# Attention and two MLPs on one core: the transposes of the units that Pool splits stand one step later in SP's order, and the softmax weights get a fifth buffer

## The chip, the core and the metric

The kernel runs on one core of a Trainium2 chip. Six instruction streams work side by side and meet at semaphores: PE (matrix multiplications, with PEld for its weight loads), DVE (vector work), ACT (activations, and DMAs that it issues), POOL (vector work on a third engine) and SP, which in this kernel only issues DMAs. Each stream keeps its order: an instruction that waits holds up all that stands behind it in the same stream. The metric is the time of one execution on the device in microseconds, the median of the runs.

## The reference

Three stages follow each other: attention with a learned bias on the scores, an MLP with the largest of three products, and a gated MLP. Sizes: 4 batches, 8 heads, 576 positions, head size 64; 2304 tokens of 512; inner sizes 768 and 1536.

```python
scores = scale * np.matmul(q, k.transpose(0, 1, 3, 2))
scores = scores + bias.transpose(2, 0, 1)[None, :, :, :]
scores = scores - np.max(scores, axis=-1, keepdims=True)
attn = np.exp(scores)
attn = attn / (np.sum(attn, axis=-1, keepdims=True) + 1e-09)
attn_out = np.matmul(attn, v)
h = np.maximum(np.maximum(x @ w1, x @ w2), x @ w3)   # x: attn_out, heads side by side
x = h @ w_out
gate = 1.0 / (1.0 + np.exp(-(x @ w_gate)))
out = gate * (x @ w_val) @ w_out2
```

## The kernel before, in words

Precision comes from pairs of 16-bit numbers: a float32 value is scaled and split into a high part `hi` and a rest `lo`, and a product takes three matmuls (`mm3`, L797).

**Units and steps.** The 32 heads go in 16 pairs P. A pair has 10 units: five row tiles (four of 128 rows, one of 64) for each of its two heads, alternating. Unit u has position u mod 10 in its pair: position 0 and 1 are tile 0 of the two heads, 2 and 3 tile 1, and so on. The loop over `u` makes one step for each unit, and every step emits work for units of different age. For unit x: scores on PE (`emit_S`, L617 and L618), at step x the sum with the bias and the row's maximum on DVE (`emit_E`, L637) and the exponential on ACT (`emit_X`, L643), at x+1 the reciprocal of the row's sum, then the split. In between the step issues a load of bias rows on ACT's DMA queue (`load_bias`, L519, for unit u+3), takes some products of the first MLP of the batch before (`feed`, L797, with their evacuation on ACT at L818 and on DVE at L820) and prepares later pairs (`prep`: loads of q, k, v, their split, the transposes of q and k by DMA at L411 and the swapped copy of k on DVE at L421 and L422). Order is thus written out by hand: each engine gets its instructions in the order in which the steps emit them.

**The split of the softmax weights.** From unit 40 on, the weights of a unit are split into a buffer `ph` (128 rows, twice 576 numbers of 16 bits); there are `NPH` buffers. For most units ACT writes `hi` at step x+1 (`emit_hi`, L662) and DVE writes `lo` at x+2 (`emit_lo`, L677). For the units at positions 2 and 5 (and 8 as well for units below 80) Pool does the float32 work (`by_pool`): it scales the row at x+1 (L659), ACT copies `hi` at x+2 (`emit_hi2`, L668) and Pool subtracts at x+3 (L674). These 28 units are called Pool's units here, the other 92 plain.

**The transpose T(x).** A full `ph` is turned by one DMA transpose on SP into `pt` (`emit_T`, L702): at step x+2 for a plain unit, at x+4 for one of Pool's. When it has landed, the `ph` buffer is free. Buffers are handed out in the order in which the program released them. The product with v (`emit_V`, L756) reads `pt`: units 0 to 3 of a pair at step 11 counted from the pair's first unit, units 4 to 9 at step 15.

Before unit 40 none of this is used (PE transposes there), and after the loop come the rest of the first MLP and the whole gated MLP (L1177 to L1217).

Of the kernel before, what the change touches and what calls it, by code (L numbers as in the profile page):

```python
# [13 lines left out]
BF16 = mybir.dt.bfloat16  # L14
# [14 lines left out]
FIRST_MOE = 6  # L29
OUT_AT = 6  # L30
QLEAD, QEARLY = 16, 6
NBI, NPH, NE, NVH = 3, 4, 4, 4
ESC = 16384.0
DOWN = 2.0 ** -15
DOWN2 = 2.0 ** -15
# [29 lines left out]
def tile_kernel(ctx, tc, q, k, v, w1, b1, w2, mw1, mw2, mw3, mwo, gw, vw, ow, xtab, masks, out):  # L65
# [3 lines left out]
    F1 = mw1.shape[1]  # L69
# [91 lines left out]
    with tc.manual_schedule():  # L161
# [8 lines left out]
        wpool = wp1.enter_context(tc.tile_pool(name="wpool", bufs=1))  # L170
# [1 line left out]
        hT = wpool.tile([128, 2, K1, S], F16, tag="hT", name="hT")  # L172
        xTs = [wpool.tile([128, 2 * KC, S], F16, tag=f"xT{i}", name=f"xT{i}") for i in range(2)]
        mt = wp1.enter_context(tc.tile_pool(name="mt", bufs=2))
        junk_v = wpool.tile([128, 640], BF16, tag="junk_v", name="junk_v")
        junk_x = junk_v[:, :S]
        junk_w = wpool.tile([128, F1], BF16, tag="junk_w", name="junk_w")


        def w_in(i):  # L180
# [330 lines left out]
        bias_t, e_t, ph_t, l_t, r_t, pt_t = {}, {}, {}, {}, {}, {}  # L511
# [133 lines left out]
        def emit_r1(u):  # L645
            m = rows[units[u][1]]
            r_t[u] = p4.tile([128, 1], F32, tag="r", name="r")
            nc.vector.tensor_scalar(r_t[u][:m], l_t.pop(u)[:m], 1e-9, 1.0 / ESC, op0=ALU.add, op1=ALU.mult)

        def by_pool(u):  # L650

            return u % 10 in ((2, 5, 8) if u < 20 * PPB else (2, 5)) and not by_pe(units[u][0])
# [42 lines left out]
        def emit_T(u):  # L695
            n, it = units[u]
            m = rows[it]
            g, i0 = (0, 0) if it < 2 else (1, 2)
            if it == i0:
                pt_t[n, g] = p1.tile([128, 9, (256, 320)[g]], F16, tag=f"pt{g}{n % 2}", name="pt")  # L700
            c0 = 128 * (it - i0)
            nc.sync.dma_start_transpose(out=pt_t[n, g][:, :, c0:c0 + m], in_=ph_t.pop(u)[:m].rearrange("p a s -> p (a s)"))  # L702
# [222 lines left out]
        def at_step(u, off):  # L925
            return [u - off] if 0 <= u - off < NU else []

        for u in range(NU + 7):
# [23 lines left out]
            tiny()  # L952
            for x in at_step(u, 1):
                emit_r1(x)
            for x in at_step(u, 4):
                if by_pool(x):
                    emit_T(x)
            for x in at_step(u, 2):
                emit_hi2(x)
                if not (by_pe(units[x][0]) or by_pool(x)):  # L960
                    emit_lo(x)
                    emit_T(x)
# [311 lines left out]
```

## Time and profile before

| | us |
|---|---|
| median of 3 runs | 1090.01 (1089.54 to 1098.89) |
| the profiled execution | 1105.99 |
| its span, first to last instruction | 1104.2 |
| units 40 to 159 with their tails (185 to 590 us of the span) | 405.0 |
| rest of the first MLP and gated MLP (590 us to the end) | 514.2 |
| PE busy in the whole span | 1001.4 (91%) |
| DVE busy | 691.0 (63%) |
| ACT busy | 550.3 (50%) |
| POOL busy | 190.5 (17%) |

A row of the timeline gives the start, the duration, the engine, the line, the operation with the tiles it writes and reads, and in brackets how long the engine sat idle before it and what ended that. An engine name with a q (SPq, ACTq) marks an instruction of the issuing stream, such as the issue of a DMA.

### The profile page before, as it was taken

The page shows a single profiled execution, that of the slowest core. Times are in us where ns is not written, and L with a number is a line of the kernel's source. Part 1 is how long each engine was busy: PE and PEld are TensorE (multiplying, and loading weights), DVE is VectorE, ACT ScalarE, POOL GpSimd, SP SyncE. Part 2 cuts the span into 40 slices and gives each one's busy share as a digit, 9 for nine tenths or more (in the row PEclk, how much of TensorE's full clock was granted, in tenths as well). Part 3 has the DMA queues.
Part 4 walks back from the last instruction along what each step waited for, and adds up shares of the span by engine and source line. Part 5 has one row for each costly group of instructions (what it writes and reads, how often), then busy time and mean ns, then how long its engine had stood idle before and what let it go on. Part 6 is the DMA issues. An engine that isn't in the chain of part 4 may idle for free.

```text
span 1104.2 us, 20184 instructions
## 1 busy us (share of the span) xinstructions
PE 1001.4 (91%) x7620; PEld 660.0 (60%) x7620; DVE 691.0 (63%) x1764; ACT 550.3 (50%) x1089; POOL 190.5 (17%) x199
## 2 busy tenths in 40 slices
PE   5977899778987889987999998998999999999998
PEld 2223454556664566655777776777764676777753
DVE  6997878888976887876884876778620221222210
ACT  6998778657675666765664435544410111111100
POOL 1003454434432233212330110000000000000000
PEclk9999999999898998988999999999999999999999
DMA  7898979999999999979994332323001000000001
GB/s 212 295 264 235 207 201 220 263 220 195 209 202 196 200 201 186 250 170 194 183 172 121 105 112 61 113 94 116 2 1 39 11 20 11 10 11 10 11 20 39
DMA packets 242957, 148.53 MB, mean 135 GB/s; under 512 B 183084, under 2 KB 214060, under 8 KB 242860
## 3 DMA queue, kind: packets, MB, share of 16 engines
q1 hardware_dynamic: 221472, 104.76, 45.5%
q10 hardware_dynamic: 21388, 42.48, 14.5%
q8 instruction: 60, 0.98, 0.4%
q14 instruction: 37, 0.30, 0.1%
HBM read 89.53 MB, written 15.34 MB: 95 GB/s over the span
## 4 chain that ended last, share of the span: by engine, by line
PE 52%; DVE 20%; DMA 12%; ACT 7%; issue 6%; POOL 1%; SPq 1%; ACTq 1%; DVEq 0%; POOLq 0%
PE po L1212 13%; PE mm L797 12%; PE pg L797 8%; PE pvl L797 8%; DMA pt<-ph 7%; PE s L797 3%; PE s L617 3%; DVE xT L543 2%; PE mm L756 2%; PE t L690 2%; ACT ph L662 2%; PE mm L752 1%; DVE e L637 1%; DVE gT L1187 1%; DVE wf L93 1%
## 5 line engine op out<-in xcount | busy, mean ns | idle before, releaser
L797 PEld LDWEIGHTS <-slot 128*128 128x128 f16 x2304 | 224.7, 101 | 106.1 <-issue 40.1
L797 PE MATMUL mm<-xT,slot 128*128 128x288 f16 x1512 | 220.8, 302 | 25.8 <-ACT hm L818 19.7
L1212 PE MATMUL po<-OW,gT 128*128 128x512 f16 x648 | 141.3, 379 | 0.0
L797 PEld LDWEIGHTS <-GW 128*128 128x128 f16 x1152 | 112.7, 98 | 41.7 <-issue 9.0
L797 PEld LDWEIGHTS <-VW 128*128 128x128 f16 x1152 | 112.2, 98 | 28.2
L643 ACT ACTIVATE e<-e,mx 128x576 f32<-128x576 f32 (+1 forms) x120 | 92.6, 771 | 45.4 <-DVE mx L637 39.0
L797 PE MATMUL pg<-x,GW 128*128 128x288 f16 x864 | 113.3, 288 | 0.5 <-DVE x_e L154 0.5
L797 PE MATMUL pvl<-x,VW 128*128 128x288 f16 x864 | 111.7, 286 | 0.0
L1212 PEld LDWEIGHTS <-gT 128*128 128x128 f16 x648 | 63.4, 98 | 74.8
L1177 ACT ACTIVATE sg<-pg,ug 128x576 f32<-128x576 f32 x48 | 35.5, 739 | 144.7 <-PE pg L797 131.1
L677 DVE SCALAR_TENSOR_TENSOR ph<-e,r,ph 128x576 f16<-128x576 f32 (+1 forms) x92 | 82.3, 895 | 39.1 <-ACT ph L662 38.9
L1184 DVE SCALAR_TENSOR_TENSOR sg<-pvl,sg 128x576 f32<-128x576 f32 x48 | 36.2, 754 | 108.5 <-PE pvl L797 107.6
L637 DVE CUSTOM_DVE_ANT_0 e<-s,bias 128x576 f32<-128x576 f32 (+1 forms) x120 | 89.4, 745 | 6.6 <-DMA bias<-bias_d 4.7
L662 ACT ACTIVATE ph<-e,r 128x576 f16<-128x576 f32 (+1 forms) x92 | 71.1, 773 | 32.9 <-DMA pt<-ph 26.0
L1186 ACT CAST gT<-sg 128x576 f16<-128x576 f32 x48 | 32.2, 672 | 107.4 <-DVE sg L1184 107.4
L617 PE MATMUL s<-k,kq 128*128 128x512 f16 (+1 forms) x160 | 63.9, 400 | 19.7 <-DVE k L422 19.7
L552 PE MATMUL bo<-xT,w2blk 128*32 128x512 f32 x192 | 61.2, 637 | 18.7 <-DVE xT L543 14.9
L617 PE MATMUL s<-kq 128*128 128x512 f16 (+1 forms) x160 | 64.9, 406 | 8.6 <-DVE mx L637 5.7
L1217 DVE TENSOR_TENSOR ob<-po,uo 128x512 f32<-128x512 f32 x16 | 11.1, 691 | 96.8 <-PE po L1212 96.8
L797 PE MATMUL mm<-hT,slot 128*128 128x288 f16 x504 | 66.2, 286 | 0.4 <-DVE xT L763 0.4
L826 POOL TENSOR_TENSOR hT<-hm,hT 128x576 f16<-128x576 f32 x24 | 39.2, 1632 | 113.3 <-ACT hT L825 105.9
L1187 DVE TENSOR_TENSOR gT<-sg,gT 128x576 f16<-128x576 f32 x48 | 36.4, 758 | 34.9 <-ACT gT L1186 34.9
(203 smaller groups left out, 1642.8 us busy)
## 6 DMA issues: line engine op xcount, KB each, us to landing
bias<-bias_d ACTq DMA_DIRECT2D x128, 288.0 KB, 3.9
bias_d<-x SPq DMA_DIRECT2D x36, 288.0 KB, 4.7
x<-in_moe_w_dram SPq DMA_DIRECT2D x12, 768.0 KB, 7.2
w<-in_moe_w_gate_dram SPq DMA_DIRECT2D x12, 512.0 KB, 3.7
w<-in_moe_w_val_dram SPq DMA_DIRECT2D x12, 512.0 KB, 3.6
w<-in_moe_w_out_dram SPq DMA_DIRECT2D x12, 512.0 KB, 3.4
bias<-bias_d ACTq DMA_DIRECT2D x32, 144.0 KB, 4.9
out_dram<-ob SPq DMA_DIRECT2D x36, 128.0 KB, 2.3
```

What stands on the lines that cost most here:

```text
L552: nc.tensor.matmul(bo[32 * g:32 * g + 32, 0:512], lhsT=lhsT, rhs=hs[4 * ti + g][:, :, 0:128], start=True, stop=True, tile_position=(0, 32 ...
L617: nc.tensor.matmul(ps[:m, 0:512], lhsT=qs, rhs=kk[:, 0:4], start=(j == 0), stop=(j == 1))
L637: nc.vector.tensor_tensor_reduce(e[:m], ps[:m, :S], bias_t.pop(u)[:m], -1.0, 3.0e38, ALU.add, ALU.min, mx[:m])
L643: nc.scalar.activation(e_t[u][:m], e_t[u][:m], AF.Exp, scale=-1.0, bias=x_t.pop(u)[:m], accum_out=l_t[u][:m])
L662: nc.scalar.activation(ph_t[u][:m, 0], e_t[u][:m], AF.Copy, scale=r[:m])
L677: nc.vector.scalar_tensor_tensor(ph[:m, 1], e_t.pop(u)[:m], r_t.pop(u)[:m], ph[:m, 0], op0=ALU.mult, op1=ALU.subtract)
L797: nc.tensor.matmul(ps[hf][:, :HS], lhsT=W(wp, kk), rhs=X(xp, kk)[:, hf * HS:(hf + 1) * HS], start=(first and i == 0), stop=(last and i == 2))
L826: nc.gpsimd.tensor_tensor(hT[:, 1, m], hm, hT[:, 0, m], op=ALU.subtract)
L1177: nc.scalar.activation(hm3(sg), pg[:, :, :HS], AF.Sigmoid, scale=ugm)
L1184: nc.vector.scalar_tensor_tensor(hm3(sg), pvl[:, :, :HS], DOWN2, hm3(sg), op0=ALU.mult, op1=ALU.mult)
L1187: nc.vector.tensor_tensor(gT[:, 1, m, c0:c0 + S], sg, gT[:, 0, m, c0:c0 + S], op=ALU.subtract)
L1212: nc.tensor.matmul(po[:, 0, :], lhsT=gT[:, gi, kk, 128 * ct:128 * ct + 128], rhs=OW[:, wi, kk], start=(i == 0), stop=(i == 3 * K2 - 1))
```

## The change

Three edits. `NPH` goes from 4 to 5. The room comes from one area less for results that nobody reads: `junk_v` becomes a part of `junk_w`. And `emit_T` of Pool's units moves from step x+4 to x+5, still ahead of the plain transposes of its step. Because unit 7 now comes ahead of unit 5, the first of a `pt` buffer's units to be issued, whichever it is, takes the buffer.

```diff
-NBI, NPH, NE, NVH = 3, 4, 4, 4
+NBI, NPH, NE, NVH = 3, 5, 4, 4
@@
-        junk_v = wpool.tile([128, 640], BF16, tag="junk_v", name="junk_v")
+        junk_w = wpool.tile([128, F1], BF16, tag="junk_w", name="junk_w")
+        junk_v = junk_w[:, :640]
         junk_x = junk_v[:, :S]
-        junk_w = wpool.tile([128, F1], BF16, tag="junk_w", name="junk_w")
@@ in emit_T
-            if it == i0:
+            if (n, g) not in pt_t:
                 pt_t[n, g] = p1.tile([128, 9, (256, 320)[g]], F16, tag=f"pt{g}{n % 2}", name="pt")
@@ in the loop over u
-            for x in at_step(u, 4):
+            for x in at_step(u, 5):
                 if by_pool(x):
                     emit_T(x)
```

The order of PE, DVE, ACT and POOL is the same row by row. What moves is SP's order. First SP in pair 9 (units 90 to 99), steps 94 to 101. The buffers `ph_4536` (unit 92, Pool's), `ph_4539` (93), `ph_4585` (94), `ph_4688` (95, Pool's), `ph_4691` (96), `ph_4732` (97), `ph_4788` (98) and `ph_4836` (99) stand in this order before:

```order
L411 DMA_TRANSPOSE kq_4544<-R_4354 128x10x128
L702 DMA_TRANSPOSE pt_4495<-ph_4539 128x9x128
L359 DMA rqk_118<-in_k_dram 128x2x256
L360 DMA rqk_118<-in_k_dram 64x2x64
L411 DMA_TRANSPOSE kq_4621<-R_4354 128x10x128
L702 DMA_TRANSPOSE pt_4453<-ph_4536 128x9x128
L702 DMA_TRANSPOSE pt_4640<-ph_4585 128x9x128
L702 DMA_TRANSPOSE pt_4640<-ph_4691 128x9x128
L702 DMA_TRANSPOSE pt_4783<-ph_4688 128x9x128
L702 DMA_TRANSPOSE pt_4783<-ph_4732 128x9x128
L702 DMA_TRANSPOSE pt_4640<-ph_4788 128x9x64
```

And the same place now, where the buffers' numbers are lower by one or two (`ph_4535` is unit 92, `ph_4584` unit 94, `ph_4687` unit 95, `ph_4731` unit 97):

```order
L411 DMA_TRANSPOSE kq_4543<-R_4353 128x10x128
L702 DMA_TRANSPOSE pt_4494<-ph_4538 128x9x128
L359 DMA rqk_117<-in_k_dram 128x2x256
L360 DMA rqk_117<-in_k_dram 64x2x64
L411 DMA_TRANSPOSE kq_4620<-R_4353 128x10x128
L702 DMA_TRANSPOSE pt_4638<-ph_4584 128x9x128
L702 DMA_TRANSPOSE pt_4452<-ph_4535 128x9x128
L702 DMA_TRANSPOSE pt_4638<-ph_4690 128x9x128
L702 DMA_TRANSPOSE pt_4783<-ph_4731 128x9x128
L702 DMA_TRANSPOSE pt_4783<-ph_4687 128x9x128
L702 DMA_TRANSPOSE pt_4638<-ph_4786 128x9x64
```

T(92) has changed places with T(94), and T(95) with T(97); each Pool transpose is one place later and the plain one one place earlier. In pairs 4 to 7 T of position 8 moves in the same way behind T of the next pair's unit 0.

Second ACT in steps 98 and 99 of the same pair, with the semaphores that a row waits for (DMAHW: a DMA that has landed). Before:

```order
L662 ACTIVATE ph_4732<-e_4674,r_4727 128x576 [waits DMAHW6_49,DVE_49,Activation_49]
L818 ACTIVATE hm_4764<-mm_4662,fac_1850 128x288 [waits PE_49]
L818 ACTIVATE hm_4764<-mm_4667,fac_1850 128x288 [waits PE_49]
L643 ACTIVATE e_4767,l_4769<-e_4767,mx_4768 64x576 [waits DVE_49]
L519 DMA bias_4772<-bias_d_60 128x576 [waits DMAHW7_49,DMAHW5_49]
L662 ACTIVATE ph_4788<-e_4715,r_4781 64x576 [waits DVE_49,Activation_49]
```

and now:

```order
L662 ACTIVATE ph_4731<-e_4672,r_4726 128x576 [waits DMAHW1_49,DVE_49,Activation_49]
L818 ACTIVATE hm_4763<-mm_4660,fac_1849 128x288 [waits PE_49]
L818 ACTIVATE hm_4763<-mm_4665,fac_1849 128x288 [waits PE_49]
L643 ACTIVATE e_4766,l_4768<-e_4766,mx_4767 64x576 [waits DVE_49]
L519 DMA bias_4771<-bias_d_60 128x576 [waits DMAHW6_49,DMAHW5_49]
L662 ACTIVATE ph_4786<-e_4714,r_4780 64x576 [waits DVE_49,Activation_49]
```

The rows are the same; `hi` of unit 97 waits for another transpose than before (T(92) before, T(93) now), and the load of bias rows behind it waits in both for T(94), whose semaphore it takes over.

## Rows read from the trace of the kernel before

**Rows 1.** Windows view: engines' busy us (instructions), then PEclk, DMA share, GB/s.
```profile
185.00:590.00 405.00, 352.31 (x2920) 243.80 (x2919) 322.70 (x894) 263.92 (x561) 129.12 (x120) 0.93 1.05 200
590.00:1104.20 514.20, 499.06 (x3604) 348.82 (x3602) 216.61 (x472) 137.35 (x244) 9.10 (x6) 0.99 0.16 47
```
**Rows 2.** Waits view of PE, 185 to 590 us: total us, times, longest.
```profile
PE mm L797 <- ACT hm L818: 19.7, 6, 5.1
PE s L617 <- DVE k L422: 19.7, 13, 3.5
```
**Rows 3.** Waits view of ACT, same stretch.
```profile
ACT ph L662 <- DMA pt<-ph: 26.0, 14, 4.2
ACT ph L668 <- DMA pt<-ph: 8.8, 5, 2.6
```
**Rows 4.** Timeline, pair 9: Pool's subtraction of unit 92, T(92) and T(94).
```profile
365.51 1.28 POOL L674 TENSOR_TENSOR ph<-e,ph 128x576 f16<-128x576 f32 x1 [1.30 <-DMA bias<-bias_d]
374.54 3.42 SPq L702 DMA_TRANSPOSE pt<-ph  x1
378.06 2.56 SPq L702 DMA_TRANSPOSE pt<-ph  x1
```
**Rows 5.** Tile view of `pt`: all transposes T, min/median/max of issue in ns, then landing.
```profile
L702 SPq DMA_TRANSPOSE pt<-ph x120: 1199/1729/4258, 187.3 to 582.5; - x120
DMA to landing us min/median/max: 2.9/4.9/8.8
```
**Rows 6.** Timeline of ACT: eight writes of `hi` that waited for a buffer.
```profile
244.85 0.78 ACT L662 ACTIVATE ph<-e,r 128x576 f16<-128x576 f32 x1 [1.98 <-DMA pt<-ph]
309.52 0.78 ACT L662 ACTIVATE ph<-e,r 128x576 f16<-128x576 f32 x1 [1.54 <-DMA pt<-ph]
319.38 0.77 ACT L662 ACTIVATE ph<-e,r 128x576 f16<-128x576 f32 x1 [2.88 <-DMA pt<-ph]
343.13 0.77 ACT L662 ACTIVATE ph<-e,r 128x576 f16<-128x576 f32 x1 [2.44 <-DMA pt<-ph]
381.75 0.78 ACT L662 ACTIVATE ph<-e,r 128x576 f16<-128x576 f32 x1 [2.59 <-DMA pt<-ph]
415.23 0.77 ACT L662 ACTIVATE ph<-e,r 128x576 f16<-128x576 f32 x1 [4.21 <-DMA pt<-ph]
510.55 0.78 ACT L662 ACTIVATE ph<-e,r 128x576 f16<-128x576 f32 x1 [1.34 <-DMA pt<-ph]
518.06 0.77 ACT L662 ACTIVATE ph<-e,r 128x576 f16<-128x576 f32 x1 [3.62 <-DMA pt<-ph]
```
**Rows 7.** Timeline of PE: the idle time next behind each of those eight.
```profile
247.60 0.38 PE L617 MATMUL s<-k,kq 128*128 128x512 f16 x1 [2.79 <-DVE k L422]
312.27 0.38 PE L617 MATMUL s<-k,kq 128*128 128x512 f16 x1 [1.58 <-DVE k L422]
321.74 0.16 PE L130 MATMUL s<-vmx,ones 128*128 128x1 bf16 x1 [1.18 <-ACT junk_v L371]
346.12 3.18 PE L797 MATMUL mm<-xT,slot 128*128 128x288 f16 x12 [3.97 <-ACT hm L818]
382.96 1.90 PE L797 MATMUL mm<-xT,slot 128*128 128x288 f16 x12 [1.75 <-ACT hm L818]
416.45 3.19 PE L797 MATMUL mm<-xT,slot 128*128 128x288 f16 x12 [3.92 <-ACT hm L818]
513.72 0.38 PE L617 MATMUL s<-k,kq 128*128 128x512 f16 x1 [1.38 <-DVE k L422]
519.27 3.19 PE L797 MATMUL mm<-xT,slot 128*128 128x288 f16 x12 [4.36 <-ACT hm L818]
```
**Rows 8.** Timeline of ACT: the longest wait of a copy `hi` (Pool's unit), with the load ahead.
```profile
472.42 0.35 ACTq L519 DMA_DIRECT2D bias<-bias_d  x1
472.87 0.67 ACT L668 CAST ph<-e 128x576 f16<-128x576 f32 x1 [2.58 <-DMA pt<-ph]
```
**Rows 9.** Windows view, 5 us behind one of those idle times.
```profile
345.00:350.00 5.00, 3.88 (x15) 2.03 (x15) 3.90 (x17) 3.10 (x6) 0.68 (x1) 0.50 1.29 192
```

## The prediction

> **What bounds the kernel now.** I read the windows first. Between 185 and 590 us PE is busy 352.3 of 405.0 us, behind that 499.1 of 514.2 [rows 1]. The change touches only units from 40 on, so only the first of these stretches can move, and there PE is the busiest engine (DVE 322.7, ACT 263.9): PE sets the pace and loses 405.0 − 352.3 = 52.7 us by idling. The waits of PE say for whom: 19.7 us for ACT's evacuation of a product (L818) and 19.7 us for DVE's copy of k (L422) [rows 2]. Both are works that come late because something ahead of them on their engine was late. The waits of ACT show that something: 26.0 us in 14 writes of `hi` and 8.8 us in 5 copies `hi` of Pool's units, all for a transpose that still held the `ph` buffer, 34.8 us together [rows 3].
>
> Why is the transpose late? In pair 9 Pool ended unit 92 at 366.79 (365.51 + 1.28), but T(92) began only at 374.54 and T(94) behind it at 378.06 [rows 4]. The time between is not a wait for Pool: SP was issuing the loads of q and k, the two transposes of q and k, and T(93), which stand ahead in its order. An issue of T occupies SP for 1.2 to 4.26 us, 1.73 in the middle, and the landing comes 4.9 us (2.9 to 8.8) after it began [rows 5]. So SP has a jam at positions 4 to 6 of every pair, and T of position 2 stands at its end.
>
> Who suffers can be followed at the same place. ACT came to `hi` of unit 97, sat idle 2.59 us, and went on at 381.75, the fifth row there [rows 6]: with four buffers that unit gets the one that T(92) releases. Right behind it in ACT's order stands the evacuation L818, for which PE sat idle 1.75 us until 382.96, again the fifth row [rows 7]. Eight such writes of `hi` (units 57, 77, 80, 87, 97, 107, 136 and 137) have an idle time of PE next behind them, of 1.18 to 4.36 us; where it is L422, the chain goes from `hi` on ACT to `lo` on DVE, and the copy of k stands behind that `lo`.
>
> **The change part by part.**
>
> *Fifth buffer and place of T.* Buffers go round in the order of release, so I counted releases. Before, a unit at position 7 takes the buffer of T(2) (unit 97 that of T(92)), one at position 0 that of T(5). With one buffer more and T(2) behind T(4), position 7 takes that of T(3), and T(2)'s comes to position 9. T(93) stands well ahead of T(92) on SP, so it has landed before ACT comes to unit 97, and position 9 is written two units later than position 7. For units 57, 77, 87, 97, 107 and 137 the wait was for T(2), for unit 80 for T(75), for unit 136 for the plain T(133), which is now T(131). I take all eight waits as gone: 1.98 + 1.54 + 2.88 + 2.44 + 2.59 + 4.21 + 1.34 + 3.62 = 20.6 us of ACT [rows 6].
>
> *The rest of ACT's waits.* 34.8 − 20.6 = 14.2 us stay in my sum. The five copies `hi` (8.8) are of another kind: the longest, 2.58 us up to 472.87, has a load of bias rows started at 472.42 in the middle of it [rows 8]. That load waits until the DMA that used its semaphore last, here a T, has landed, and a fifth buffer doesn't change that. The other six writes of `hi` are under 1.6 us each (5.4 together), with no idle time of PE that I could put behind them. Bounds: nothing, or all 14.2.
>
> *What the wait on the semaphore does to the eight.* Behind `hi` of unit 97 stands, after L818, the load of bias rows that waits for T(94), before and now. If T(94) stayed where it was, ACT would gain the evacuation and then stop at that load. This is what the second edit is good for: T(94) takes the place of T(92), so it begins at 374.54 instead of 378.06, 3.5 us earlier [rows 4], more than the 2.59 us that ACT gains. T(92) then begins some 2.6 us later (the issue of T(94), 2.56); its reader, unit 99, is two units away.
>
> *What PE gets.* Each idle time of PE can shrink by no more than ACT's wait ahead of it and no more than itself, so I take the smaller of each pair [rows 6, 7]: 1.98 + 1.54 + 1.18 + 2.44 + 1.75 + 3.92 + 1.34 + 3.62 = 17.8 us.
>
> *The clock.* After the idle time that ended at 346.12 twelve matmuls took 3.18 us [rows 7], and the window behind it has a granted clock of 0.50 [rows 9], that is 1.2 GHz where 1.00 is 2.4. PE was busy 3.88 of these 5 us, so 1.9 us of it would fall away at the full level. The two other idle times of that size (3.92 and 4.36) have the same slow matmuls behind them (3.19 us for twelve each). Three times 2 us: 6 us. Bounds: 0, where other waits keep PE idle for as long, and 10, counting the shorter idle times too.
>
> *The areas for unused results.* The writes into `junk_w` are ACT's, and three of DVE's at units below 40, where the order shows no new wait between engines. Price 0; the cover is ACT's own order, and uncovered it would be a wait of one such instruction, below 1 us.
>
> *What is moved past.* T(2) and T(5) stand behind one more T. Their reader is `emit_V`, four and five steps later than their place; T(92) landed at the latest when unit 97 went on, at 381.75, and with 2.6 us more it is still well ahead of step 101. No load on SP comes later by it: a moved T only gives its place to others (in pair 4 to a load of weights too). Price 0.
>
> Sum: 17.8 + 6 = 23.8 us of the profiled execution, 1105.99 → 1082.2. The runs without a profile have a median of 1090.01, 16.0 us less. The stretch behind 590 has only 15.1 us of idle PE, and what the change touches is the first, so I choose to put those 16 us down to its waits: 52.7 there are 36.7 in an ordinary run, 0.70 of it. The gain scales alike: 23.8 × 0.70 = 16.6, and 1090.0 − 16.6 = 1073.4. I forecast **1074 us**.
>
> By the page DMA: Bandwidth & Descriptors of the Trainium skill (section Issuing engines are not separate DMA queues) the time on the sequencer to initiate a DMA is usually small relative to the DMA itself; then the place in SP's order would be worth nothing, and the outcome is the first rival's, 1082 us. The trace speaks against it here: an issue of 1.73 beside a landing of 4.9 is more than a third [rows 5].
>
> **The rivals.**
>
> *The jam only moves.* SP's issue is what is scarce, and T(94) lands no earlier for being issued earlier. ACT is then let through at `hi` and stopped at the load of bias rows, one step later. Against it: T(94) had a whole place of 3.5 us to gain. For it: the five copies of `hi` show such stops already [rows 8]. Price: the idle times behind L818 shrink (2.44 + 1.75 + 3.92 + 3.62 = 11.7) but the next step gives about half of that back, and the clock half of its 6: about 9 us profiled, 6 to 8 without; 1082.
>
> *The waits belong to the profile.* If without it transposes land sooner, few of the eight waits exist in a timed run, and the 16 us are these. Then 36.7 us of idle time are of other causes and the gain is a rest of 3 to 6 us; 1085.
>
> *The moved transposes become the late ones (slower).* Position 9 waits for T(2), which now lands later. Landings reach 8.8 us against 4.9 in the middle [rows 5], so one T can be 3.9 us late. It decides from about 2 us a pair: in 12 pairs that is 24 us, as much as I take away. With 3.9 us in each pair the profiled time would rise by 47 − 24 = 23 us, some 16 without a profile: 1106. Against it: unit 99 is written two units behind unit 97, and a step takes over 3 us (405 us for 120 units).
>
> **How the numbers follow.** My forecast 0.57, the jam only moves 0.22, the waits belong to the profile 0.13, slower 0.08. About 1% (10.9 us) is what a measurement can tell from no change. The forecast's own range is 1060 (30 us: the 17.8 and the clock's 10 unscaled, and 2 of the 14.2) to 1079 (11 us, where a third of the pairs wait elsewhere). The two rivals at 1082 and 1085 are inside of 1%, the slower one is split at 1101. With the edge to 1088 the range holds both; it leaves out the slower rival and the tails, 2 in 10. Faster by over 1%: 0.58 (the forecast and a little of the first rival); within 1%: 0.35; slower: 0.07.
>
> **What would show it.** In the changed kernel's profile ACT's wait for transposes at L662 should fall from 26.0 us to below 8 and that at L668 stay near 8.8; PE's wait for L818 should fall from 19.7 to below 9; PE's idle time between 185 and 590 from 52.7 to about 35, and no window there at 0.50 behind a unit at position 7. T(4) should begin right behind the second transpose of q and k. I am wrong if waits of that size appear at the loads of bias rows (L519) or at units of position 9, or if L818 and L422 still hold PE for 30 us or more while L662's wait is gone: then DVE or SP, and not the buffer, set the pace.

## The result, and the profile after

The changed kernel takes 1084.58 us (median of 18 executions, 1076.81 to 1101.99); the kernel before, run beside it and with the three executions known at the forecast, 1097.88 us (18 executions, 1088.25 to 1104.80). The ratio is 0.989, 95% interval 0.987 to 0.992: faster by about 1%, 13.3 us between the medians, where 16.6 us were forecast. (The ratios here leave out executions more than 1.5% above the fastest of their kernel; in the set with the k copies one step earlier a single execution of before, 1081.15 us, makes these nine of 23, so that the ratios of that set lie 0.3 to 0.6% above those of all medians, which stand beside them.) The profiled execution went from 1105.99 to 1089.23 us, by 16.8 us, where the sum had 23.8.

Nearly all of it lies where the forecast put it. The windows view, cut at the times when DVE begins its pass L637 on units 48, 84 and 159, before:

```profile
199.46:324.66 125.20, 106.02 (x878) 73.59 (x876) 105.50 (x283) 82.20 (x176) 48.88 (x41) 0.93 1.09 224
324.66:577.38 252.72, 221.28 (x1832) 153.04 (x1830) 199.96 (x563) 162.98 (x343) 74.75 (x72) 0.93 1.06 193
577.38:1104.20 526.82, 511.68 (x3721) 358.88 (x3718) 220.50 (x482) 144.44 (x262) 9.10 (x6) 0.99 0.17 48
```

and after, columns as in [rows 1]; the last line here is the first stretch of [rows 1]:

```profile
200.21:318.35 118.14, 102.12 (x873) 71.77 (x871) 105.74 (x284) 82.28 (x177) 47.07 (x41) 0.97 1.12 233
318.35:559.64 241.29, 215.64 (x1831) 151.12 (x1830) 199.15 (x564) 161.87 (x341) 73.88 (x72) 0.96 1.12 204
559.64:1087.40 527.76, 513.97 (x3725) 359.91 (x3722) 220.48 (x482) 144.49 (x262) 9.09 (x6) 0.99 0.17 48
185.00:590.00 405.00, 361.30 (x3079) 254.30 (x3080) 332.93 (x921) 272.16 (x582) 128.90 (x122) 0.97 1.07 207
```

What comes ahead of unit 48 and behind unit 159 is the same to 1 us; between them 377.9 us became 359.4, by 18.5. A window less PE's busy time is PE's idle time: 19.2 + 31.4 = 50.6 us before, 16.0 + 25.7 = 41.7 after, 9.0 less. PE's busy time on the same work fell from 327.3 to 317.8 us, 9.5 less, and the granted clock rose from 0.93 to 0.97 and 0.96. So between these two profiles the idle time gave 9.0 us where 17.8 were forecast, and the clock 9.5 where 6 were. Each is a single profile, and the one of before was slower than any of its 18 executions. In the kernel with the place alone, which the experiments below find no faster than before, the same stretch has these two windows, cut at the same units:

```profile
196.94:322.15 125.21, 103.03 (x878) 72.23 (x876) 103.92 (x284) 82.45 (x176) 47.62 (x41) 0.96 1.14 221
322.15:563.56 241.41, 215.97 (x1827) 150.80 (x1826) 198.19 (x564) 162.99 (x343) 74.01 (x72) 0.95 1.07 203
```

PE is idle there for 22.2 + 25.4 = 47.6 us and busy for 319.0. So most of the 9.0 us of idle time stands against this profile too (5.9 are left), but of the 9.5 us of the clock only 1.2.

The waits of PE between 185 and 590 us, after, answer to [rows 2]:

```profile
PE s L617 <- DVE k L422: 13.3, 10, 3.0
PE mm L797 <- DVE xT L763: 8.4, 8, 2.8
PE s L617 <- DVE mx L637: 6.3, 4, 2.1
PE mm L797 <- ACT hm L818: 6.1, 5, 2.3
PE mm L756 <- ACT e L643: 1.9, 1, 1.9
PE mm L756 <- DMA pt<-ph: 1.2, 1, 1.2
PE mm L756 <- DVE r L657: 1.1, 1, 1.1
```

The two waits that the forecast was about fell from 39.4 to 19.4 us, 20.0 less: a little more than the 17.8. But others came. Two of them stood before with

```profile
PE mm L797 <- DVE xT L763: 4.7, 5, 2.5
PE s L617 <- DVE mx L637: 4.2, 2, 2.1
```

and are 5.8 us longer; the waits at the V product (L756), 4.2 us in these three lines, were not there at all. About half of the 20.0 was given back, between these two profiles.

ACT's waits, to be held against [rows 3]:

```profile
ACT ph L668 <- DMA pt<-ph: 6.2, 3, 2.7
ACT ph L662 <- DMA pt<-ph: 6.2, 3, 3.1
```

26.0 us became 6.2. The longest of the three at L662 shows that it is no wait for a buffer any more. ACT in the changed kernel, pair 9, and PE behind it:

```profile
387.20 0.34 ACTq L519 DMA_DIRECT2D bias<-bias_d  x1
387.64 0.78 ACT L662 ACTIVATE ph<-e,r 128x576 f16<-128x576 f32 x1 [3.13 <-DMA pt<-ph]
```

```profile
390.33 1.90 PE L797 MATMUL mm<-xT,slot 128*128 128x288 f16 x12 [1.10 <-ACT hm L818]
```

ACT had finished its exponential at 384.51; the load of bias rows that stands ahead of the write of `hi` began at 387.20, when T(97) had landed (387.18). (The load that waits for T(94), three units earlier, did not stop ACT: T(94) landed at 376.55, and when the load began at 376.62, ACT was still at an exponential.) In the kernel before, ACT lost 2.59 us in this pair at `hi` of unit 97 [rows 6] and PE 1.75 [rows 7]; now ACT loses 2.69 us at a load, and PE 1.10. Added up over the timeline of 185 to 590 us (each gap over 0.15 us ahead of such a load), ACT's stops at bias loads were 20.6 us in 15 before and are 26.6 us in 19. That they grew is not shown by these sums: with four buffers and the place alone they are 18.1 us, with four buffers and only the shared area 31.3.

### The profile page after: what moved, and what is told of

Its sections match the earlier page's. It is cut to its first block, busy times and chain, and to the rows that moved or that the text cites. A ratio compares the mean times of both kernels' runs of the same rounds, so it can differ in the third digit from the quotient of the medians.

```text
span 1087.4 us, 20167 instructions
## 1 busy us (share of the span) xinstructions
PE 994.8 (91%) x7620; PEld 658.0 (61%) x7620; DVE 690.3 (63%) x1764; ACT 549.7 (51%) x1089; POOL 188.0 (17%) x199
## 4 chain that ended last, share of the span: by engine, by line
PE 54%; DVE 20%; DMA 10%; ACT 7%; issue 4%; SPq 1%; ACTq 1%; POOL 1%; DVEq 0%; POOLq 0%
PE po L1212 13%; PE mm L797 12%; PE pg L797 8%; PE pvl L797 8%; PE s L797 3%; PE s L617 3%; DMA pt<-ph 3%; PE mm L756 2%; PE t L690 2%; DMA rqk<-in_q_dram 2%; PE mm L752 2%; DVE e L637 2%; DVE xT L543 1%; DMA rqk<-in_k_dram 1%; DVE gT L1187 1%
## 5 line engine op out<-in xcount | busy, mean ns | idle before, releaser
L797 PEld LDWEIGHTS <-slot 128*128 128x128 f16 x2304 | 221.4, 99 | 91.7 <-issue 29.3
L797 PE MATMUL mm<-xT,slot 128*128 128x288 f16 x1512 | 212.9, 294 | 17.4 <-DVE xT L763 8.4
L643 ACT ACTIVATE e<-e,mx 128x576 f32<-128x576 f32 (+1 forms) x120 | 92.5, 771 | 52.1 <-DVE mx L637 48.1
L637 DVE CUSTOM_DVE_ANT_0 e<-s,bias 128x576 f32<-128x576 f32 (+1 forms) x120 | 89.5, 746 | 10.2 <-DMA bias<-bias_d 7.9
L1186 ACT CAST gT<-sg 128x576 f16<-128x576 f32 x48 | 32.2, 672 | 107.3 <-DVE sg L1184 107.3
L662 ACT ACTIVATE ph<-e,r 128x576 f16<-128x576 f32 (+1 forms) x92 | 71.0, 771 | 18.1 <-DMA pt<-ph 6.2
L552 PE MATMUL bo<-xT,w2blk 128*32 128x512 f32 x192 | 60.6, 620 | 18.5 <-DVE xT L543 14.9
L617 PE MATMUL s<-k,kq 128*128 128x512 f16 (+1 forms) x160 | 62.9, 393 | 13.3 <-DVE k L422 13.3
L1217 DVE TENSOR_TENSOR ob<-po,uo 128x512 f32<-128x512 f32 x16 | 11.1, 691 | 96.8 <-PE po L1212 96.8
L617 PEld LDWEIGHTS <-kq 128*128 128x128 f16 (+1 forms) x320 | 32.6, 102 | 39.9 <-issue 17.4
```

The lines of the kernel that those rows point to most:

```text
L552: nc.tensor.matmul(bo[32 * g:32 * g + 32, 0:512], lhsT=lhsT, rhs=hs[4 * ti + g][:, :, 0:128], start=True, stop=True, tile_position=(0, 32 ...
L617: nc.tensor.matmul(ps[:m, 0:512], lhsT=qs, rhs=kk[:, 0:4], start=(j == 0), stop=(j == 1))
L637: nc.vector.tensor_tensor_reduce(e[:m], ps[:m, :S], bias_t.pop(u)[:m], -1.0, 3.0e38, ALU.add, ALU.min, mx[:m])
L643: nc.scalar.activation(e_t[u][:m], e_t[u][:m], AF.Exp, scale=-1.0, bias=x_t.pop(u)[:m], accum_out=l_t[u][:m])
L662: nc.scalar.activation(ph_t[u][:m, 0], e_t[u][:m], AF.Copy, scale=r[:m])
L797: nc.tensor.matmul(ps[hf][:, :HS], lhsT=W(wp, kk), rhs=X(xp, kk)[:, hf * HS:(hf + 1) * HS], start=(first and i == 0), stop=(last and i == 2))
```

## The experiments

Each is given with its edit of the changed kernel unless it says otherwise; medians are of 6 to 12 executions, the kernel before was run beside each set (medians 1097.79, 1094.88, 1095.13 and 1097.00 us).

**The parts of the change.** The buffer alone (Pool's transposes at x+4, as before):

```
-            for x in at_step(u, 5):
+            for x in at_step(u, 4):
```

> Five buffers, the transposes of Pool's units where they were before (step x+4). My theory (both edits are needed): position 7 now takes the buffer of T(3) and is let through, but ACT stops right behind it at the load of bias rows that waits for T(4), and position 8 waits for T(2). ACT's wait for transposes at L662 falls from 26.0 us to 8 to 15, its idle time at the bias loads (L519) rises, PE's wait for L818 falls by about half (19.7 to 8 to 12), time 4 to 8 us under before (ratio 0.993 to 0.996). Rival A (the buffer alone does it, the place in SP's order is worth nothing): the same time as the changed kernel, ratio 0.989 plus or minus 0.002. Rival B (the order does it): ratio 1.000.

Measured: 1087.96 us (six executions), ratio 0.989 (0.983 to 0.994), of the medians 0.991. By the ratio that is the gain of the whole change, by the medians 9.8 us of its 13.3. The theory's time, 4 to 8 us, lies below both, though the interval still touches it. Its waits came as it said:

```profile
ACT ph L662 <- DMA pt<-ph: 11.1, 6, 3.6
PE mm L797 <- ACT hm L818: 10.5, 5, 5.1
```

and ACT's gaps ahead of bias loads rose to 39.7 us in 26.

The place alone (four buffers):

```
-NBI, NPH, NE, NVH = 3, 5, 4, 4
+NBI, NPH, NE, NVH = 3, 4, 4, 4
```

> Four buffers, the transposes of Pool's units at step x+5. My theory: position 7 now waits for T(4), which lands where T(2) landed before, and position 8 for T(2), which lands later: ACT's wait at L662 stays at 22 to 32 us and the time is 0 to 4 us over before (ratio 1.000 to 1.004). Rival A (buffer alone): ratio 1.000. Rival B (the order does it): ratio 0.989 to 0.992, with PE's wait for L818 under 10 us.

Measured: 1095.67 us, ratio 1.000 (0.996 to 1.003), as expected. ACT still waits for buffers, a little less than the 22 us and more of the theory:

```profile
ACT ph L662 <- DMA pt<-ph: 19.9, 17, 3.6
```

(Its profiled execution had a span of 1090.9 us and was the fastest of its twelve: one profile, 13 us below that of before, would have told a gain that isn't there.)

The area for unused squares alone (both edits above together):

> Only the area for unused results is shared; four buffers and the old place of the transposes. Every theory: no change, ratio 0.998 to 1.002. If it is under 0.995 or over 1.005, the shared area has an effect of its own that none of the theories holds.

Measured: 1098.60 us, ratio 0.998 (0.994 to 1.002): no change, as expected.

**One step more.** All 28 transposes of Pool's units at x+6:

```
-            for x in at_step(u, 5):
+            for x in at_step(u, 6):
```

> Five buffers, the transposes of Pool's units yet one step later (x+6). My theory: little more is won or lost, since position 9 doesn't wait for T(2) any more but a load of bias rows (unit 103 in pair 10's counting, issued at step 100) does: within 3 us of the changed kernel (ratio to before 0.986 to 0.993). The slower rival (a moved transpose becomes the late one): 8 us or more over the changed kernel (ratio 0.996 or above), with waits for transposes at L519, L662 or in the products with v (L756).

Measured: 1104.49 us, ratio 1.006 (1.002 to 1.009), some 18 us more than the changed kernel; "within 3 us" fell. The waits of PE at the V product, from its timeline:

```profile
232.49 3.95 PE L756 MATMUL mm<-pt,vh 128*64 128x320 f16 x28 [8.06 <-DMA pt<-ph]
270.10 3.94 PE L756 MATMUL mm<-pt,vh 128*64 128x320 f16 x28 [4.01 <-DMA pt<-ph]
307.26 3.94 PE L756 MATMUL mm<-pt,vh 128*64 128x320 f16 x28 [4.77 <-issue]
342.51 3.29 PE L756 MATMUL mm<-pt,vh 128*64 128x320 f16 x28 [4.32 <-DMA pt<-ph]
```

They add up to 21.2 us, all in pairs 4 to 7, all in the product of step 15. Only these pairs have a Pool unit at position 8. At x+6 its transpose is issued in step 14 and the product that reads it stands in step 15. The changed kernel has the beginnings of it, at x+5:

```profile
262.56 2.26 PE L756 MATMUL mm<-pt,vh 128*64 128x320 f16 x28 [1.10 <-DVE r L657]
293.63 2.09 PE L756 MATMUL mm<-pt,vh 128*64 128x320 f16 x28 [1.23 <-DMA pt<-ph]
323.41 2.19 PE L756 MATMUL mm<-pt,vh 128*64 128x320 f16 x28 [1.89 <-ACT e L643]
```

(the three landings of T(58), T(68) and T(78), at 262.46, 293.58 and 323.32, are each within 0.1 us of the product's start, whatever releaser the profile names). Three runs took the positions apart; the edit is one rule:

```
-            for x in at_step(u, 5):
-                if by_pool(x):
-                    emit_T(x)
+            for o in (6, 5, 4):
+                for x in at_step(u, o):
+                    if by_pool(x) and o == (6 if x % 10 == 8 else 4):
+                        emit_T(x)
```

This one, position 8 at x+6 and the others at x+4:

> Five buffers, the transposes of positions 2 and 5 at x+4, only the four of position 8 at x+6. Theory: these four make all of the loss that all 28 at x+6 made: the V product of step 15 of pairs 4 to 7 waits for them, four PE gaps of 4 to 8 us at L756, 18 to 22 us in sum, nothing in pairs 8 to 15; 1102 to 1108 us, ratio 1.004 to 1.009. Rival (the loss comes from hi copies and bias loads behind all late transposes, spread over twelve pairs): four of 28 make a seventh of it, 1087 to 1091 us, ratio 0.989 to 0.994.

Measured: 1098.68 us, ratio 1.002 (0.999 to 1.006), 10.7 us above the kernel with all at x+4 (medians of two sets): between the two expectations; the interval touches the theory's range and not the rival's seventh. By the ratios to the kernel before of each set (1.002 and 0.989) the difference is some 15 us. The gaps stand where the theory put them, in pairs 4 to 7 alone, and are a little shorter, 16.4 us together:

```profile
227.91 3.12 PE L756 MATMUL mm<-pt,vh 128*64 128x320 f16 x28 [3.68 <-DMA pt<-ph]
263.12 3.66 PE L756 MATMUL mm<-pt,vh 128*64 128x320 f16 x28 [2.49 <-DMA pt<-ph]
...
298.95 4.01 PE L756 MATMUL mm<-pt,vh 128*64 128x320 f16 x28 [4.67 <-DMA pt<-ph]
335.37 3.42 PE L756 MATMUL mm<-pt,vh 128*64 128x320 f16 x28 [5.60 <-DMA pt<-ph]
```

The mirror image, `4 if x % 10 == 8 else 6`, position 8 at x+4 and the other 24 at x+6:

> Five buffers, the four transposes of position 8 at x+4, the 24 of positions 2 and 5 at x+6. Theory: these have room to spare before the V products that read them (the closest gap is behind position 8), so moving them by two steps costs nothing and brings nothing: within 4 us of the kernel with five buffers and all at x+4 (1088 us), ratio 0.983 to 0.992, no wait of PE for pt at L756. Rival (a later transpose holds a buffer and a completion semaphore longer, and hi copies or bias loads stop for it): ACT's stops at L662, L668 and L519 grow by 15 us or more, 1096 to 1105 us, ratio 0.998 to 1.006.

Measured: 1085.97 us, ratio 0.990 (0.987 to 0.994): moved by two steps these transposes cost nothing and bring nothing that can be told within some 4 us, as the theory said. (One wait for pt of 5.3 us at L756 was in its profile, against the expectation of none.)

And `4 if x % 10 == 8 else 5`, the changed kernel without its three small gaps:

> The changed kernel with the transposes of position 8 (units 48, 58, 68, 78) back at x+4; positions 2 and 5 stay at x+5. Theory: with five buffers the only late transpose is that of position 8, for which the V product of step 15 waits in the changed kernel's pairs 5 to 7 (PE gaps of 1.10, 1.23 and 1.89 us at L756). These gaps go, nothing else moves: 4 us less than the changed kernel, about 1080 us, ratio to before 0.984 to 0.988, and no wait of PE for pt at L756 in the loop. Rival (place in SP's order is worth nothing at either step): 1084 to 1088 us, ratio 0.989 to 0.991.

Measured: 1084.13 us, ratio 0.990 (0.985 to 0.995). The gaps for pt are gone from its trace, and the time is the changed kernel's. Time and ratio lie in the rival's range, and the interval reaches into the theory's: no gain that can be told from none.

**What the rest of PE's waits are worth.** The largest that is left, the wait for the k copies, taken away by making them one step earlier:

```
-                lo, tr, sw = ((8, 10), 10, 14) if Pq else ((7, 8), 8, 11)
+                lo, tr, sw = ((8, 10), 10, 13) if Pq else ((7, 8), 8, 11)
```

> The changed kernel with the k copies of DVE (L421, L422) one step earlier, at position 13 in place of 14. The largest wait of PE that is left is the S product's for that copy, 13.3 us in 10 stops. Theory (idle time of PE that is taken away comes off the time one for one, as the prediction's step assumed): it falls below 4 us, nothing of it comes back, 1073 to 1077 us, ratio 0.977 to 0.982. Rival (half and more comes back at the next wait, as in the changed kernel: DVE then waits for the k transposes and its maxima and xT come later): PE's idle falls by 5 us or less, 1080 to 1086 us, ratio 0.985 to 0.991.

Measured: 1087.22 us, ratio 0.997 (0.993 to 1.000), of the medians 0.993: by either no faster than the changed kernel. PE's waits:

```profile
PE mm L797 <- ACT hm L818: 13.9, 7, 4.5
PE s L617 <- DVE mx L637: 9.5, 10, 2.1
PE mm L797 <- DVE xT L763: 6.2, 8, 1.9
PE s L617 <- DVE r L648: 3.3, 2, 1.9
```

The wait for L422, 13.3 us, is gone, as is its line; DVE has it now, for the transposes of k:

```profile
DVE k L421 <- DMA kq<-R: 13.7, 9, 2.7
```

and PE has waits for L818, for the maxima and for L648 that are 7.8 + 3.2 + 3.3 us longer. Its idle time between units 48 and 159 is 43.3 us (41.7 in the changed kernel): none of the 13.3 us came off the time, and "one for one" was wrong here. The rival named the mechanism: the copy now stands ahead of the landing of the transposes that it reads, and DVE has a stop of its own that it didn't have before. So the edit moved a wait more than it took one away, and the time was a little above the rival's 1080 to 1086.

**Whether ACT's stops at bias loads took the place.** The loads of units 40 to 159 from Pool's queue, where by the built order they wait for no transpose:

```
-            nc.scalar.dma_start(t[:rows[it]], bias_d[h, 128 * it:128 * it + rows[it], :])
+            (nc.gpsimd if u >= 40 else nc.scalar).dma_start(t[:rows[it]], bias_d[h, 128 * it:128 * it + rows[it], :])
```

> The changed kernel with the 120 bias loads of units 40 to 159 issued from Pool's queue instead of ACT's; by the built order they then wait for no transpose. Theory A (new wait): in the changed kernel ACT's stops at bias loads (26.6 us idle ahead of L519 in 185 to 590) took the place of the buffer stops and hold PE as those did; they go, PE's idle in the loop falls from 43 to about 33 us, 1074 to 1079 us, ratio 0.978 to 0.984. Rival B (slack): ACT's stops there only move its slack, which it spends at L643 for DVE instead (50 us there grows by 15 or more); 1081 to 1087 us, ratio 0.986 to 0.992. Rival C: Pool, in order behind its own waits, issues the loads late, DVE's wait for a bias at L637 grows from 7.9 to over 20 us, 1092 us or more, ratio above 0.995.

Measured: 1084.93 us (six executions, 1075.48 to 1097.55), ratio 0.986 (0.980 to 0.993), of the medians 0.991. Time and ratio lie in B's range; the interval reaches into A's. ACT's wait at L643 did not grow as B had it (43.5 us against 46.8). Its profiled execution is the fastest of all, and there PE's idle time is 19.0 + 16.8 = 35.8 us, near what A said:

```profile
196.29:318.46 122.17, 103.13 (x858) 71.43 (x856) 113.73 (x284) 81.85 (x176) 63.33 (x77) 0.94 1.05 226
318.46:546.54 228.08, 211.33 (x1849) 150.48 (x1848) 208.10 (x564) 162.97 (x343) 111.62 (x146) 0.99 1.05 215
```

The same with position 8 at x+4:

> The changed kernel with both of the last edits: the transposes of position 8 at x+4 (positions 2 and 5 at x+5) and the bias loads of units 40 to 159 on Pool's queue. Theory: what is left of waits for transposes in the changed kernel are its V products of pairs 5 to 7 (4.2 us of PE gaps) and ACT's bias loads (PE idle 43 to 36 us in the kernel that moved them alone); both go, PE's idle in 185 to 590 is 31 to 36 us, 1073 to 1080 us, ratio 0.977 to 0.985. Rival (only the fifth buffer counts, what remains is slack): 1083 to 1088 us, ratio 0.988 to 0.992.

Measured: 1093.49 us, ratio 1.002 (0.997 to 1.006), of the medians 0.998. Both expectations fell: even the buffer's gain is gone. PE's idle time between units 48 and 159 is 24.8 + 25.5 = 50.3 us, that of before, though ACT's wait for buffers at L662 is only 3.6 us. DVE is busy for 324.5 us (304.9 in the changed kernel), and PE waits 20.4 us for its k copy (13.3):

```profile
197.43:322.56 125.13, 100.33 (x852) 70.04 (x851) 113.36 (x283) 82.35 (x176) 63.77 (x77) 0.96 1.08 220
322.56:566.08 243.52, 217.99 (x1854) 153.85 (x1853) 211.09 (x564) 162.35 (x343) 111.36 (x146) 0.96 1.07 203
```

The kernel before, with this edit alone:

> The kernel before (four buffers, Pool's transposes at x+4) with only its bias loads of units 40 to 159 moved to Pool's queue. Theory (the buffer comes first): ACT's waits for a buffer stay, 20 us or more at L662, and PE's idle in 185 to 590 stays at 45 us or more; 1090 to 1097 us, ratio 0.994 to 1.001. Rival (a stop of ACT is a stop, whatever it waits for: before loses 20.6 us of ACT idle ahead of L519, as many as at the eight buffer waits of [rows 6]): the gain of the fifth buffer comes from this edit too, 1083 to 1088 us, ratio 0.987 to 0.992.

Measured: 1100.21 us (six executions), ratio 1.010 (1.003 to 1.017), of the medians 1.005. No gain, and above the theory's range; ACT's waits for buffers are all there,

```profile
ACT ph L662 <- DMA pt<-ph: 26.5, 17, 4.5
```

so the theory was right that the buffer comes first, and the edit seems to cost something itself. To see why the two kernels before it disagreed, the loads were moved only from unit 84 on, where Pool has two units of ten (`u >= 84` in the line above), on the changed kernel:

> The changed kernel with the bias loads of units 84 to 159 on Pool's queue, those of units 40 to 83 left on ACT's. The two kernels with all 120 loads on Pool disagree (0.986 and 1.002 of before); in both the steps 48 to 84, where Pool has three units of ten, were no faster than in the changed kernel (122 and 125 us, against 118), and one of them was 13 us faster in the steps 84 to 159 (228 us against 241). Theory A (ACT's stops at bias loads hold PE, and only a full Pool queue in the first part spoils it): steps 48 to 84 as in the changed kernel, 116 to 120 us, steps 84 to 159 in 226 to 234 us, 1071 to 1079 us, ratio 0.975 to 0.984. Rival B (ACT's stops there are slack, taken again at the exponentials of L643, and the fast profile was one lucky draw): steps 84 to 159 in 236 to 246 us, 1082 to 1090 us, ratio 0.987 to 0.996.

Measured: 1086.09 us, ratio 0.991 (0.987 to 0.994), and

```profile
195.33:312.28 116.95, 99.03 (x875) 70.62 (x873) 105.59 (x284) 82.08 (x176) 49.70 (x44) 1.00 1.12 234
312.28:553.21 240.93, 215.36 (x1836) 150.95 (x1835) 207.89 (x563) 162.04 (x343) 110.76 (x146) 0.96 1.05 204
```

And on the kernel with positions 2 and 5 at x+6:

> Five buffers, position 8 at x+4, positions 2 and 5 at x+6, and the bias loads of units 84 to 159 on Pool's queue. The kernel without the last edit took 1086 us (0.990) and 235 us for the steps 84 to 159. Theory A: ACT's stops at bias loads go, steps 84 to 159 in 222 to 230 us, 1072 to 1080 us, ratio 0.976 to 0.985. Rival B: no change to the kernel without the edit, 1083 to 1090 us, ratio 0.987 to 0.995. Rival C (a late transpose of positions 2 and 5 is only free as long as ACT stops often; without those stops the V products of step 11 wait for it): PE gaps at L756 for pt of 5 us or more in the steps 84 to 159, above 1090 us.

Measured: 1089.09 us, ratio 0.992 (0.989 to 0.995). Rival B's times in both: ACT's gaps ahead of bias loads between 185 and 590 us fell from 26.6 to 5.4 us in the first of them, and PE's idle time between units 48 and 159 stayed, 17.9 + 25.6 = 43.5 us against 41.7. Taking the stops away brought no time. That they are slack is not shown by it: ACT's wait at L643, where B had the slack spent, is 40.1 us against 46.8, and the edit makes DVE's work between units 84 and 159 longer by 8.7 us (207.9 against 199.2), which may have eaten a gain. Why the kernel with all loads on Pool's queue was as fast as it was, and the one with position 8 at x+4 so slow, stays open; they ran in different sets. No version was shown to beat the changed kernel.

## Why the prediction was right and wrong

**What bounds the kernel: right.** The change moved the time between units 48 and 159 and nothing behind it.

**Eight waits of ACT go, 20.6 us: right, and more.** 26.0 us of waits at L662 became 6.2, of which the longest, 3.13, is a stop at a load. That they shrink with the fifth buffer is shown by the run with the buffer alone (11.1) and the one with the place alone (19.9). Of the other signs set down, PE's wait for L818 came out below 9 (6.1) and ACT's at L668 near 8.8 (6.2), but PE's idle time between 185 and 590 us at 405.0 − 361.3 = 43.7 and not at about 35.

**Both edits are needed: not borne out.** The step said that ACT, let through at `hi`, would stop at the load that waits for T(94) unless T(94) came 3.5 us earlier. The stops are there as it said: with the buffer alone ACT's gaps ahead of bias loads are 39.7 us in 26, with both edits 26.6. But ratio against ratio, 0.989 and 0.989, they cost nothing that can be measured (medians against medians 3.5 us), and 21 us less of them brought nothing in a third kernel. The place in SP's order was worth nothing that can be told from none here, and on the edge of costing something: the sum had it at 0 because the readers stand four and five steps later, which is so at positions 2 and 5. At position 8 of pairs 4 to 7 the reader is the product of step 15, two steps behind step 13, and I had not looked there. The slower rival (the moved transposes become the late ones) had the mechanism, but named a buffer at position 9, not the V product, and one step more was needed for it to decide.

The page DMA: Bandwidth & Descriptors of the Trainium skill (section Issuing engines are not separate DMA queues), by which the issue is usually small beside the transfer, would have made the place worth nothing; for one step, and for two at positions 2 and 5, the runs agree with that outcome (0.989 and 0.990 against 0.989), though not with the small share, 1.73 of 4.9 us [rows 5]. What the place costs at position 8, 10.7 us in the median, is not the time of an issue but the distance to a reader.

**What PE gets, 17.8 us: the step that failed.** I took the smaller of ACT's wait and PE's wait in each pair as gained. PE's waits for L818 and L422 did shrink, by 20.0 us, but PE's idle time between units 48 and 159 fell by 9.0 (in the kernel with the buffer alone by 8.0). The rest came back as waits for xT, the maxima and the V product.

How much comes back is less sure than that the idle time fell short. In the other profiles with four buffers (shared area alone; place alone; before with loads on Pool's queue) the two waits are 41.7, 32.2 and 33.8 us together and the idle time 54.0, 47.6 and 49.0. In those with five that differ from the changed kernel only in where Pool's transposes stand, and were about as fast (buffer alone; position 8 at x+4; that and the others at x+6), the waits are 25.8, 27.5 and 21.5 us and the idle time 42.6, 40.0 and 41.8. Between any profile with four buffers and any of these with five the idle time drops by 5 to 14 us, never by 17.8, and the two waits by 5 to 22.

A reading that fits is that between two units PE, ACT and DVE are all close behind each other, so that a wait that goes lets PE come to its next operand earlier than that is ready. The run with the k copies points the same way, 13.3 us away and none of it gained, but there the edit itself gave DVE a new stop. The 16.4 us of waits for pt at the V product, put in by moving four transposes, cost 10.7 us by the medians and raised PE's idle time by 9.1 (51.7 against 42.6 with the buffer alone), so part of a wait that is put in is taken back as well. ACT loses there too:

```profile
ACT xT L762 <- PE mm L756: 28.8, 11, 8.1
```

7.2 us with the buffer alone: while PE waits for pt, ACT waits for PE. None of this shows the reason; it is argued.

**The clock, 6 us: right in kind, its size not settled.** The stretches at 0.50 behind the three longest of those waits [rows 7, 9] are gone in the profile after, and PE's busy time on the same work fell by 9.5 us, inside the bounds of 0 and 10. Over 185 to 590 us the trace of before has ten stretches at 0.50, 55 us together, that of after six with 24 us. But the profile with the place alone, a kernel with no gain, has seven with 34 us and PE's busy time at 319.0, 8.3 below that of before; so how much of the 9.5 belongs to the change stays open. The longest stretch that is left stands behind a wait for the k copy of 3.02 us:

```profile
340.00:345.00 5.00, 4.59 (x19) 2.58 (x19) 3.20 (x16) 2.38 (x5) 0.80 (x1) 0.50 1.17 186
```

**The base and the scale: wrong.** The three executions had a median of 1090.01; 18 have 1097.88, so the time forecast came out 7.9 us low from this alone. And that the 16.0 us by which the profiled execution was slower were waits of the profile nothing bears out: profiled executions of the changed versions lie on both sides of their medians, from 9 us below (loads on Pool's queue) to 11 above (shared area alone); of the 16.0 us 8.1 are left, as much as single executions of before differ from their median (1088 to 1105), and the profiled execution of the changed kernel is 4.7 us above its median. Scaling the sum by 0.70 for them was without ground. It happened to take off what the failed step had put on too much: without it the forecast of the change would have been 23.8 instead of 16.6 us, against 13.3.

**The rivals.** "The jam only moves" named two things that were seen: a stop that moved to a load of bias rows, in pair 9, and a next step that gave part back. But what came back stands at xT, the maxima and the V product, and that the stops at the loads caused it no run shows. Its 6 to 8 us were too few; the waits for L818 shrank by 13.6 us and not by half of 11.7. "The waits belong to the profile" ended at nearly the time measured, 1085, for the wrong reason: its gain of 3 to 6 us is below the interval (0.8 to 1.3% of 1097.88, 9 to 14 us).

## What to carry to other kernels

Do not add up removed waits as if each came off the time: here the change took about 9 us off PE's idle time where 17.8 were added up, and another edit that took 13.3 us of waits away gained nothing, because DVE stopped in its place. Before summing, ask of each wait what the waiting engine will wait for next, and what the engine that it waited for will wait for. A place in an issuing order is free as long as every reader is far: look for the nearest reader among all the positions, not at the usual one. A median of three whose executions spread over 9 us is no base for an effect of 1%, and neither is the difference of one profile to another: one kernel without any gain had a profile 13 us below that of before.

## What the runs showed of the hardware

Moving loads to Pool's queue made DVE slower, which I had not expected. In the kernel that moved them only from unit 84 on, DVE is busy for 105.6 us between units 48 and 84, as in the changed kernel (105.7), and for 207.9 against 199.2 behind that. With all of them moved, an issue took Pool 567 ns in the middle, where one of ACT's took 327; Pool's busy time between units 48 and 159 rose from 121.0 to 175.0 us, DVE's from 304.9 to 321.8 for the same work. The copies of L452 (DVE, vh) show it, in the changed kernel and in the one with all loads on Pool's queue (min/median/max in ns):

```profile
L452 DVE COPY vh<-vh x24: 251/253/1286, 199.2 to 559.1; 64x320 f16<-64x320 f16 x24
```

```profile
L452 DVE COPY vh<-vh x24: 251/700/1378, 195.3 to 546.0; 64x320 f16<-64x320 f16 x24
```

The page SBUF — State Buffer of the Trainium skill (section Who interferes with whom) says that a DVE copy can take the port pair that it shares with GpSimd, and that whoever comes second is blocked. The trace agrees in that such copies go from 253 to 700 ns when Pool is busier; that the port is the cause, no run here shows.

A load that waits for the landing of another engine's transpose stops the whole queue of its engine: in the changed kernel ACT stood 2.69 us up to 387.20, 0.02 us after T(97) had landed, and the write of `hi` behind it, unit 101's, waits for no transpose by the built order.
